# Copies of U and of first quarters ahead of seeds on ScalarE, p7's seed in two copies, p4's first quarter between p5's and p7's direct ones, and one check moved

## The chip, the cores and the metric

The kernel runs on one core of a Trainium2 chip. The engines in this text are TensorE (PE, with its weight loads listed as PEld), VectorE (DVE), ScalarE (ACT), GpSimd (POOL) and the queue of SyncE (SP), which issues transfers. Each engine takes its instructions strictly in the order in which they were written for it, and waits on semaphores for the work of the others. The metric is device microseconds of one execution; the kernel before took 794.69 us as the median of three runs (794.3 to 795.52).

## The reference

Two blocks follow each other. The first is attention with hashed buckets, for q, k and v of shape (4, 8, 768, 64): six sign bits of a projection give each query and key a bucket, and a score counts only where the buckets agree.

```python
scores = scale * np.matmul(q, k.transpose(0, 1, 3, 2))
scores = np.where(mask, scores, -1000000000.0)
attn = softmax(scores)            # with 1e-9 added to the sum
x = (attn @ v), heads side by side        # (4, 768, 512)
```

The second block is an MLP mixer over x. Every array is float32.

```python
h = np.maximum(xt @ w_tok1, 0.0) @ w_tok2         # xt: x with tokens last; 256 wide
u = x + h.transpose(0, 2, 1)
h2 = np.maximum(u @ w_ch1, 0.0) @ w_ch2           # 512 -> 1536 -> 512
return u + h2
```

The change lies in `np.maximum(u @ w_ch1, 0.0)`, for the last two of three parts of the tokens.

## The kernel before

The kernel has three stages: attention, the mixing of tokens, and the channels (function `channels`). In `channels` the 3072 tokens are taken in three parts `s` = 0, 1, 2 of 1024 tokens. Each part has a hidden stage (times w_ch1, then relu, into R0 to R3) and an output stage (`outputs`, times w_ch2).

Both products are formed by Winograd's variant of Strassen's scheme: seven block products p1 to p7 in the place of eight. For `s` = 1 and 2 the hidden stage applies the scheme twice. There one call of `hidden_first` (for t = 0) and two calls of `hidden_pair` (t = 1 and 2) make a part, so that `hidden_pair` runs four times in all. In a pair, p1 is computed whole and p2 to p7 are each an object of class `Smaller` with seven inner products of 128 x 256, in three methods:

- `one` forms the first inner product in PSUM and copies it to `e[:, 0]` with ScalarE (L925): the "first quarter".
- `rest` adds three more inner products in the same pair of PSUM banks. `finish` then copies the running sum U out of PSUM on ScalarE (L956), and VectorE adds it to the second and third quarters (L957) and forms the fourth (L961). The result is `e`, four quarters of 128 x 256.
- `three` forms the last three inner products, the "direct ones", and adds them to whatever stands in a given pair of PSUM banks.

So a quantity is complete when `e` and the direct ones have been added. In `hidden_pair` this is done for p6, p5 and p7 by putting a start value into the banks before `three` runs on them, the "seed". For p6 (bank pair Z) and p7 (bank pair V) the seed is `e` itself: `finish(to)` lets VectorE write the fourth quarter straight into the banks and then has ScalarE copy the first three quarters there in one copy of 128 x 768 (L963). For p5 (bank pair Y) VectorE adds `e5` and `u` into the banks (L981, function `plus`, line 1111).

Each matrix product of the program stands in the trace as two matmul instructions and two weight loads. In this text "p4's first quarter" on TensorE is thus a pair of instructions, and "p7's direct ones" are six. In the rows of the trace they can be told by what they read: p7's direct ones read `TA,WC` four times and `SW,WC` twice, p4's first quarter reads `TB,SW` twice, p5's direct ones read `TA,WC`, `TA,SW` and `second,WC` twice each.

There are eight PSUM banks, taken as four pairs. In `hidden_pair` they are named one to four: X and p3 use one, p5 and then Y use two, p2, p7 and p4 use three, Z and V use four.

The order of the work is written by hand: `tc.manual_schedule()` keeps, on each engine, the order of the program's statements, so that a statement that is moved in the text is moved on its engine's queue. Waits are put in by the framework from the tiles that are read and written. Weights for the inner products come by transfers on the SP queue; `used` issues the next one when `rest` and `three` of a quantity have both run.

One more thing is done on the side. A check (`look`: `begin_look` at L1444, `end_look` at L1452) loads one half of q or k with a transfer that POOL issues (L1462), squares it on ScalarE and adds up what lies over a bound, to decide at the end whether a careful path must run. There are 32 such loads with three under way at a time, so 35 calls drain them. The calls are spread over the hidden and output stages from the end of part 0 on; before the change there are 36, of which the last one has nothing to do.

Of the kernel before, what the change touches and what calls it, by code (L numbers as in the profile page):

```python
# [41 lines left out]
ALU = mybir.AluOpType  # L42
# [6 lines left out]
def kernel(  # L49
# [13 lines left out]
    nc = tc.nc  # L63
    P = 128
    B, NP, _, _, S = qk.shape
# [11 lines left out]
    TT = 512  # L77
# [674 lines left out]
    def channels(pool, psum, SW1, second, TA, judge):  # L752
# [7 lines left out]
        last = B * S // (2 * TT) - 1  # L760

        def copies():
            return pool.tile([P, 2 * TT], F32, name="c", tag="c", bufs=3)
# [4 lines left out]
        def bank_pair(i):  # L768
            return psum.tile([P, 2, TT], F32, name=f"b{i}", tag=f"b{i}", bufs=1)
# [91 lines left out]
        def split4(a):  # L861
            return a.rearrange("p (n t) -> p n t", n=4)
# [10 lines left out]
        def fetch_fifth(s, t):  # L873

            if t < GP:
                nc.sync.dma_start(
                    out=fifth_left().rearrange("p (i c) -> p i c", i=4),
                    in_=hidden_passed["p5"][:, :, P * t : P * t + P],
                )
# [26 lines left out]
        class Smaller:  # L906
# [11 lines left out]
                    w = hidden_left_at(h).rearrange("p (i c) -> p i c", i=7)  # L918
                    self.left = [w[:, i] for i in range(7)]

            def one(self, pair, e):

                self.ps, self.e = split4(pair.rearrange("p i n -> p (i n)")), split4(e)
                self.mm(self.ps[:, 0], 4, 0)
                nc.scalar.copy(self.e[:, 0], self.ps[:, 0])  # L925

            def three(self, pair, start=False):
# [21 lines left out]
            def mm(self, ps, left, right, start=True):  # L949
                accumulate(ps, lambda k: self.left[left], lambda k: self.b[right], [0], start)  # L950

            def finish(self, to=None):

                u = extra_flat()[:, TT // 2 * finished[0] : TT // 2 * (finished[0] + 1)]
                finished[0] = (finished[0] + 1) % 3
                nc.scalar.copy(u, self.ps[:, 0])  # L956
                nc.vector.tensor_tensor(  # L957
                    self.e[:, 1:3], self.ps[:, 1:3], u[:, None, :].to_broadcast([P, 2, TT // 2]), op=ALU.add,
                )
                last = self.e if to is None else split4(flat(to))  # L960
                nc.vector.tensor_tensor(last[:, 3], self.ps[:, 1], self.e[:, 2], op=ALU.add)  # L961
                if to is not None:
                    nc.scalar.copy(last[:, :3], self.e[:, :3])  # L963

        def parts_of(s, t):

            r = [a[:, :, t::GP].rearrange("p n i c -> p i n c") for a in R]
            h = 5 * GP * (s - 1) + 5 * t
            return r, [Smaller(h + i, name, s, t) for i, name in enumerate(SMALLER)]

        def rows(a):
            return a.rearrange("p (i n c) -> p i n c", i=2, n=2)
# [4 lines left out]
        def flat(a):  # L977
            return a.rearrange("p i n -> p (i n)")

        def plus(to, a, b):  # L980
            nc.vector.tensor_tensor(to, a, b, op=ALU.add)  # L981

        def copy_pair(to, pair):
            nc.scalar.copy(to.rearrange("p (i n) -> p i n", i=2), pair)
# [4 lines left out]
        def whole(pair, left, right, which, t):  # L989
            for i in which:  # L990
                at = P * (t + GP * i)
                accumulate(pair[:, i], lambda k: left(k)[:, at : at + P], right, range(KC))

        def opened(pair, which, s, t):
            start = TT * 2 * s
            whole(pair, lambda k: WC1[:, k], lambda k: XT[:, k, start : start + TT], which, t)
# [15 lines left out]
        def hidden_first(s, t, between):  # L1012


            r, (p2, p6, p7, p3, p4) = parts_of(s, t)
            x, z, e, y = ring
            ring[:] = [y, e, z, x]
            p1, e4, e2, e3 = [flat(output_at(i)) for i in range(4)]
            e7 = flat(q1)
            p5, e6, u = copies(), copies(), copies()  # L1020
            n = TT * 3 // 2

            X = bank_pair(x)
            opened(X, [0, 1], s, t)
            fetch_fifth(s, t + 1)
            Z, E = bank_pair(z), bank_pair(e)
            p2.one(E, e2)
            copy_pair(p1, X)
            p2.three(Z, True)
            Y = bank_pair(y)  # L1030
            whole(Y, lambda k: WC1[:, k, DCH // 2 :], lambda k: T[0][:, k], [0], t)
            plus(p1[:, :n], flat(Z)[:, :n], p1[:, :n])
            for job in between[:2]:
                job()
            p2.rest()
            whole(Y, lambda k: WC1[:, k, DCH // 2 :], lambda k: T[0][:, k], [1], t)
            p2.finish()
            copy_pair(p5, Y)
            plus(r[0], rows(p1), rows(e2))
            p6.three(X)  # L1040
            p6.one(bank_pair(z), e6)
            copy_pair(u, X)
            look()
            V = bank_pair(e)
            between[2]()
            p7.three(V, True)
            p6.rest()
            plus(p5[:, :n], flat(V)[:, :n], p5[:, :n])
            between[3]()
            p6.finish()  # L1050
            plus(u, u, e6)
            p7.one(bank_pair(x), e7)
            look()
            p3.three(Y)
            p7.rest()
            p7.finish()
            p3.one(bank_pair(z), e3)
            relu(r[0])
            p4.three(V)
            p3.rest()  # L1060
            plus(r[1], banks(Y), rows(u))
            plus(u, u, e7)
            plus(r[2][:, 0], banks(V)[:, 0], rows(u)[:, 0])
            plus(r[2][:, 1, 0], banks(V)[:, 1, 0], rows(u)[:, 1, 0])
            p3.finish()
            p4.one(bank_pair(x), e4)
            look()
            nc.scalar.copy(r[2][:, 1, 1], rows(u)[:, 1, 1])
            open_next(y, s, t)
            p4.rest()  # L1070
            plus(r[3], rows(p5), rows(u))
            p4.finish()
            plus(r[1], r[1], rows(e3))
            plus(r[2], r[2], rows(e4))
            look()
            later(r, (3, 2))

        def hidden_pair(s, t):


            r, (p2, p6, p7, p3, p4) = parts_of(s, t)
            p5 = Smaller(None, "p5", s, t)
            one, two, three, four = ring
            e2, e4, e5, e3 = [flat(output_at(i)) for i in range(4)]
            e6 = e7 = flat(q1)
            p1, u, v = copies(), copies(), copies()

            X = ahead.pop()
            p6.one(bank_pair(two), e6)
            opened(X, [1], s, t)  # L1090
            p2.one(bank_pair(three), e2)
            copy_pair(p1, X)
            p6.rest()
            p2.rest()
            Z = bank_pair(four)
            p6.finish(Z)
            p2.three(X)
            p2.finish()
            begin_look()
            p5.one(bank_pair(two), e5)  # L1100
            end_look()
            plus(r[0], banks(X), rows(e2))
            p6.three(Z)
            p7.one(bank_pair(three), e7)
            plus(u, flat(Z), p1)
            p5.rest()
            p5.finish()
            p3.one(bank_pair(one), e3)
            Y = bank_pair(two)
            plus(flat(Y), e5, u)  # L1110
            p7.rest()
            V = bank_pair(four)
            p7.finish(V)
            p3.rest()
            p5.three(Y)
            p3.finish()
            copy_pair(v, Y)
            p7.three(V)
            relu(r[0])
            plus(r[3], banks(V), rows(v))  # L1120
            p4.one(bank_pair(three), e4)
            p3.three(Y)
            relu(r[3])
            plus(r[1], banks(Y), rows(e3))
            p4.rest()
            p4.finish()
            look()
            p4.three(V)
            plus(e4, e4, u)
            plus(r[2], banks(V), rows(e4))  # L1130
            end_rows()
            if t + 1 < GP:
                open_next(one, s, t)
            else:
                ring[:] = [one, two, three, four]
            later(r, (2,))
# [5 lines left out]
        ahead, finished = [], [0]  # L1142
# [91 lines left out]
        def output_at(i):  # L1234

            at = 7 * QC * P + KC * TT * (i % 3)
            return area(i // 3)[:, at : at + KC * TT].rearrange("p (i n) -> p i n", i=KC)

        def extra_flat():
            at = 7 * QC * P + KC * TT  # L1240
            return area(1)[:, at : at + QC * TT // 2]
# [113 lines left out]
        def outputs(s):  # L1355
            sl = [slice(TT * (2 * s + i), TT * (2 * s + i) + TT) for i in range(2)]

            def add(to, a, b):
                return lambda: nc.vector.tensor_tensor(to, a, b, op=ALU.add)
# [15 lines left out]
            begin("p5")  # L1375
            combine("x", "r3", ALU.subtract, "r1", [(0, 0), (1, 0), (1, 1)])
            nc.scalar.copy(q1, ps)
            if s < last:
                look()
            q7, q57, q6, q5 = [output_at(i) for i in range(4)]  # L1380
            product(s, 1, "p5", q5, [lambda: combine("r0", "x", ALU.subtract, "r0")])
# [53 lines left out]
        def look():  # L1435
            begin_look()
            end_look()
# [192 lines left out]
```

## Time and profile before

| what | value |
|---|---|
| median of three runs | 794.69 us (794.3 to 795.52) |
| profiled execution, its own time | 795.07 us |
| its span, from the first to the last instruction | 793.2 us |
| PE busy | 785.3 us, 99% of the span |
| DVE, ACT, POOL busy | 674.4, 445.3 and 53.6 us |
| granted PE clock | 0.999 |
| the four calls of `hidden_pair` | from about 547.9, 570.4, 679.5 and 702.1 us on |

The page of a profile gives busy times and the chain of work that ended last. A row of the timeline gives the start and length in us, the engine, the line, the operation, what it writes and reads with shapes, how many instructions are merged in the row, and in brackets the idle time of that engine just before it with what ended it. Matmuls are pipelined: a matmul's recorded length overlaps the next, so that lost time on PE is read from the distances between starts.

### The profile page before, as it was taken

What the parts mean: (1) busy time and instruction counts of PE and PEld (TensorE: products, weight loads), DVE (VectorE), ACT (ScalarE), POOL (GpSimd) and SP (SyncE); (2) the same over time, 40 slices, a digit from 0 to 9 for tenths busy, and PEclk for the clock granted to TensorE, in tenths of its full rate; (3) what the DMA queues carried; (4) which work ended last, traced back from release to release, by engine and by line L of the source; (5) the groups of instructions that cost most, each with busy time, mean ns of one, the idle gap of its engine ahead of it and who ended that gap; (6) DMA issues with size and microseconds to landing.
All of it is one profiled execution on the core that took longest, in us unless ns stands there. A gap on an engine that the chain in (4) does not pass through costs nothing.

```text
span 793.2 us, 12404 instructions
## 1 busy us (share of the span) xinstructions
PE 785.3 (99%) x4721; PEld 475.2 (60%) x4721; DVE 674.4 (85%) x925; ACT 445.3 (56%) x726; POOL 53.6 (7%) x77
## 2 busy tenths in 40 slices
PE   9999999999999999999999999999999999999997
PEld 4444444444444444455544458877777887776886
DVE  5989898988987677999697789898779899878986
ACT  6688888888888886333323221327664555673111
POOL 1000000000000000011121010111000122000001
PEclk9999999999999999999999999999999999999999
DMA  4435353537452425795686995798745689720565
GB/s 164 163 123 163 123 163 123 163 125 240 148 181 88 150 47 167 216 263 111 119 279 234 347 371 164 225 302 240 250 141 197 236 236 245 232 84 0 190 172 123
DMA packets 102160, 144.85 MB, mean 183 GB/s; under 512 B 30216, under 2 KB 71888, under 8 KB 102096
## 3 DMA queue, kind: packets, MB, share of 16 engines
q1 hardware_dynamic: 93936, 119.02, 46.1%
q0 software_dynamic: 7728, 24.64, 13.6%
q8 instruction: 38, 0.62, 0.3%
q10 hardware_dynamic: 432, 0.34, 0.2%
q14 instruction: 26, 0.21, 0.1%
HBM read 101.01 MB, written 35.52 MB: 172 GB/s over the span
## 4 chain that ended last, share of the span: by engine, by line
PE 97%; DVE 2%; ACT 1%; issue 0%; ACTq 0%; DVEq 0%
PE b L780 48%; PE sc L353 20%; PE acc L407 16%; PE t L653 5%; PE t L693 5%; PE sums L431 2%; PE hp L301 1%; DVE b L981 1%; ACT b L963 0%; PE idle L470 0%; DVE second L957 0%; PE hw L325 0%; DVE q L957 0%; DVE b L961 0%; DVE second L961 0%; ACT second L956 0%
## 5 line engine op out<-in xcount | busy, mean ns | idle before, releaser
L360 ACT ACTIVATE e<-sc 128x768 f32<-128x768 f32 x192 | 154.2, 812 | 11.2 <-PE sc L353 10.8
L353 PE MATMUL sc<-qk 64*128 64x384 f32 x768 | 153.0, 484 | 0.0
L780 PE MATMUL b<-R,second 128*128 128x256 f32 (+1 forms) x612 | 150.9, 404 | 0.0
L780 PEld LDWEIGHTS b<-R,second 128*128 128x128 f32 x612 | 116.3, 190 | 31.6 <-issue 17.5
L407 PE MATMUL acc<-e,vn 128*32 128x384 f32 x1536 | 127.0, 486 | 0.0
L786 ACT COPY c<-b 128x512 f32<-128x512 f32 (+1 forms) x78 | 37.4, 488 | 156.6 <-PE b L780 142.7
L392 DVE TENSOR_TENSOR esd<-esd,e 128x768 f32<-128x768 f32 x96 | 92.0, 958 | 10.4 <-ACT e L360 0.5
L407 PEld LDWEIGHTS acc<-e,vn 128*32 128x32 f32 x1536 | 49.9, 110 | 73.9 <-issue 73.3
L353 PEld LDWEIGHTS sc<-qk 64*128 64x128 f32 x768 | 68.4, 188 | 41.8 <-issue 36.7
L780 PE MATMUL b<-XT,WC 128*128 128x256 f32 (+1 forms) x228 | 74.3, 470 | 0.0
L353 PE MATMUL sc<-bits 64*128 64x384 bf16 x384 | 62.5, 323 | 0.0
L780 PEld LDWEIGHTS b<-XT,WC 128*128 128x128 f32 x228 | 43.2, 190 | 25.9 <-issue 20.8
L388 DVE SCALAR_TENSOR_TENSOR esd<-e 128x768 f32<-128x768 f32 x32 | 30.6, 955 | 23.4 <-ACT e L360 23.4
L780 PE MATMUL b<-XT,SW 128*128 128x256 f32 (+1 forms) x156 | 43.7, 412 | 0.0
L653 PE MATMUL t<-x,W 128*128 128x512 f32 x96 | 41.8, 593 | 0.0
L353 PEld LDWEIGHTS <-bits 64*128 64x128 bf16 x384 | 18.5, 94 | 33.2 <-issue 9.4
L713 POOL DMA_DIRECT2D XT<-second x8 | 9.8, 1229 | 383.5 <-DVE second L712 361.2
L780 PEld LDWEIGHTS b<-XT,SW 128*128 128x128 f32 x156 | 29.6, 190 | 10.0 <-issue 5.1
L452 ACT COPY rec<-rec 32x384 f32<-32x384 f32 x64 | 32.6, 510 | 5.0 <-DVE rec L446 4.2
L413 ACT ACTIVATE num<-acc,vsum 128x384 f32<-128x384 f32 x32 | 18.6, 582 | 29.7 <-PE acc L407 29.3
L780 PE MATMUL b<-TA,WC 128*128 128x256 f32 (+1 forms) x92 | 34.0, 479 | 1.3 <-ACT b L963 1.3
L395 DVE TENSOR_TENSOR esd<-esd,e 128x768 f32<-128x768 f32 x32 | 30.5, 954 | 1.9
(243 smaller groups left out, 1172.5 us busy)
## 6 DMA issues: line engine op xcount, KB each, us to landing
second<-left SPq DMA_DIRECT2D x20, 768.0 KB
raw<-in_moe_w_ch SPq DMA_DIRECT2D x16, 768.0 KB
qk<-in_qk SPq DMA_DIRECT2D x15, 768.0 KB
second<-left SPq DMA_DIRECT2D x18, 576.0 KB
seen<-in_qk POOLq DMA_DIRECT2D x21, 384.0 KB, 4.8
WC<-hidden_left SPq DMA_DIRECT2D x18, 448.0 KB
vn<-in_v SPq DMA_DIRECT2D x16, 384.0 KB
vt<-in_vT SPq DMA_DIRECT2D x16, 384.0 KB
```

The source lines that it names most:

```text
L353: nc.tensor.matmul(sc[:, i, :HALF], t[rows, 1, P * c : P * c + P], t[rows, 0, qs], start=start, stop=not start,)
L360: nc.scalar.activation(e, sc[:, :, :HALF], ACT.Exp, scale=SCALE)
L388: nc.vector.scalar_tensor_tensor(self.d, es[0], NR * EPS, es[1], op0=ALU.add, op1=ALU.add,)
L392: nc.vector.tensor_tensor(self.d, self.d, e, op=ALU.add)
L395: nc.vector.tensor_tensor(self.d, self.d, self.es[-1], op=ALU.add)
L407: nc.tensor.matmul(acc[D * i + d : D * i + d + 32], vn[:, i, c, d : d + 32], e[:, i], start=(c == 0), stop=(c == NR - 1),)
L413: nc.scalar.activation(nums[self.n][:, self.half], acc, ACT.Identity, scale=-1.0, bias=vsum,)
L452: nc.scalar.copy(rec[other : other + 32, h], rec[at : at + 32, h])
L653: nc.tensor.matmul(ps, W1[:, r, P * j : P * j + P], x[:, r], start=(r == 0), stop=(r == NR - 1),)
L693: nc.tensor.matmul(ps[at], left, right, start=start, stop=True, skip_group_check=True,)
L780: nc.tensor.matmul(ps, left(k), right(k), start=start and k == ks[0], stop=stop and k == ks[-1], skip_group_check=True,)
L786: nc.scalar.copy(c, ps)
```

## The change

`finish` is split into `unite`, which copies U on ScalarE, and `add`, which holds the work of VectorE, with the fourth quarter written to a seed where one is given. The copy of the first three quarters into the seed is no longer part of it and stands in `hidden_pair`. `one` can leave its copy out, and `keep` does it later. In `hidden_pair`:

- p2's U is copied before the seed of p6 is.
- p7's seed is copied in two: the first quarter (128 x 256) right after p3's first quarter was copied, the other two (128 x 512) where the single copy stood. p3's U is copied before this second one.
- On TensorE, p4's first quarter stands between p5's direct ones and p7's direct ones. Before, it stood after p7's direct ones. Its copy to `e4` comes after that of Y to `v` on ScalarE.

The check at the end of `hidden_first` is taken out (for `s` = 1 and 2). The output stage of `s` = 1 begins with two checks in the place of one; that of `s` = 0 with one, as before. There are now 35 calls.

```diff
-            def one(self, pair, e):
+            def one(self, pair, e, now=True):
                 self.ps, self.e = split4(pair.rearrange("p i n -> p (i n)")), split4(e)
                 self.mm(self.ps[:, 0], 4, 0)
+                if now:
+                    self.keep()
+
+            def keep(self):
                 nc.scalar.copy(self.e[:, 0], self.ps[:, 0])
...
-            def finish(self, to=None):
-
-                u = extra_flat()[:, TT // 2 * finished[0] : TT // 2 * (finished[0] + 1)]
+            def unite(self):
+
+                self.u = extra_flat()[:, TT // 2 * finished[0] : TT // 2 * (finished[0] + 1)]
                 finished[0] = (finished[0] + 1) % 3
-                nc.scalar.copy(u, self.ps[:, 0])
+                nc.scalar.copy(self.u, self.ps[:, 0])
+
+            def add(self, last=None):
+
+                last = self.e if last is None else last
                 nc.vector.tensor_tensor(
-                    self.e[:, 1:3], self.ps[:, 1:3], u[:, None, :].to_broadcast([P, 2, TT // 2]), op=ALU.add,
+                    self.e[:, 1:3], self.ps[:, 1:3], self.u[:, None, :].to_broadcast([P, 2, TT // 2]), op=ALU.add,
                 )
-                last = self.e if to is None else split4(flat(to))
                 nc.vector.tensor_tensor(last[:, 3], self.ps[:, 1], self.e[:, 2], op=ALU.add)
-                if to is not None:
-                    nc.scalar.copy(last[:, :3], self.e[:, :3])
+
+            def finish(self):
+                self.unite()
+                self.add()
... in hidden_first
             plus(r[2], r[2], rows(e4))
-            look()
             later(r, (3, 2))
... in hidden_pair
             Z = bank_pair(four)
-            p6.finish(Z)
+            seed = split4(flat(Z))
+            p6.unite()
+            p6.add(seed)
+            p2.unite()
+            nc.scalar.copy(seed[:, :3], p6.e[:, :3])
             p2.three(X)
-            p2.finish()
+            p2.add()
...
             plus(u, flat(Z), p1)
+            V = bank_pair(four)
+            seed = split4(flat(V))
             p5.rest()
             p5.finish()
             p3.one(bank_pair(one), e3)
+            nc.scalar.copy(seed[:, 0], p7.e[:, 0])
             Y = bank_pair(two)
             plus(flat(Y), e5, u)
             p7.rest()
-            V = bank_pair(four)
-            p7.finish(V)
+            p7.unite()
+            p7.add(seed)
             p3.rest()
+            p3.unite()
+            nc.scalar.copy(seed[:, 1:3], p7.e[:, 1:3])
             p5.three(Y)
-            p3.finish()
+            p4.one(bank_pair(three), e4, False)
+            p3.add()
             copy_pair(v, Y)
+            p4.keep()
             p7.three(V)
             relu(r[0])
             plus(r[3], banks(V), rows(v))
-            p4.one(bank_pair(three), e4)
             p3.three(Y)
... in outputs
             nc.scalar.copy(q1, ps)
-            if s < last:
+            for _ in range(s + 1 if s < last else 0):
                 look()
```

## The prediction

> **What bounds the kernel now.** I read the page first. PE is busy 99% of the span and the chain that ended last is 97% PE, so only a stretch in which PE does not start its next matmul on time can be won, and any new one is lost whole.
>
> ```profile
> PE 785.3 (99%) x4721; PEld 475.2 (60%) x4721; DVE 674.4 (85%) x925; ACT 445.3 (56%) x726; POOL 53.6 (7%) x77
> PE 97%; DVE 2%; ACT 1%; issue 0%; ACTq 0%; DVEq 0%
> ```
>
> Next the waits of PE. In the channel stages one line ends PE's recorded idle time: the copy of a seed, four times, once in each `hidden_pair`.
>
> ```profile
> PE b L780 <- ACT b L963: 1.3, 4, 0.3
> ```
>
> 1.3 us is not the loss, since a matmul's length overlaps the next. I take the loss from the starts in the timeline of all engines, first pair of part 1:
>
> ```profile
> 558.18 0.37 ACT L956 COPY second<-b 128x256 f32<-128x256 f32 x1 [0.92 <-PE b L780]
> 558.59 0.69 DVE L957 TENSOR_TENSOR second<-b,second 128x512 f32<-128x512 f32 x1
> 559.31 0.42 DVE L961 TENSOR_TENSOR second<-b,second 128x256 f32<-128x256 f32 x1
> 559.71 1.46 PE L780 MATMUL b<-XT,SW 128*128 128x256 f32 x6
> 559.77 1.23 DVE L981 TENSOR_TENSOR b<-second,c 128x1024 f32<-128x1024 f32 x1
> 559.91 0.37 ACT L956 COPY second<-b 128x256 f32<-128x256 f32 x1 [0.92 <-PE b L780]
> 560.91 0.68 DVE L957 TENSOR_TENSOR q<-b,second 128x512 f32<-128x512 f32 x1
> 561.15 0.67 PE L780 MATMUL b<-TA,WC 128*128 128x256 f32 x2
> 561.63 0.43 DVE L961 TENSOR_TENSOR b<-b,q 128x256 f32<-128x256 f32 x1
> 562.09 0.59 PE L780 MATMUL b<-second,WC 128*128 128x256 f32 x2
> 562.15 0.80 ACT L963 COPY b<-q 128x768 f32<-128x768 f32 x1 [1.87 <-DVE b L961]
> 562.89 0.37 ACT L956 COPY second<-b 128x256 f32<-128x256 f32 x1
> 563.01 0.73 PEld L780 LDWEIGHTS b<-TA,WC 128*128 128x128 f32 x4 [0.73 <-ACT b L963]
> 563.01 1.13 PE L780 MATMUL b<-TA,WC 128*128 128x256 f32 x4 [0.33 <-ACT b L963]
> 563.98 0.59 PE L780 MATMUL b<-SW,WC 128*128 128x256 f32 x2
> ```
>
> Undisturbed, such matmuls start every 0.216 us (narrow ones; two make 0.43). From 562.09 p7's direct ones are due at 562.09 + 0.43 = 562.52, and their fifth instruction at 563.39; it starts at 563.98. So 0.59 us is lost, with the same spacing in the other three pairs. The weight load, which normally starts 0.216 ahead of its matmul, was due at 562.30 and came at 563.01, 0.71 late: 0.59 lost. At p5's direct ones (561.15) it is 0.33 late and 0.22 lost. Both say that the first 0.11 us of a late load costs nothing.
>
> The rows above it are the chain: p5's U (558.18), p5's sums, the seed Y (559.77), p7's sums, and the copy L963 for 0.80.
>
> The second loss is in the first pair after each `hidden_first`, from the timelines of ACT and PEld:
>
> ```profile
> 548.32 0.85 ACT L1444 ACTIVATE seen<-seen 128x768 f32<-128x768 f32 x1
> 550.13 0.35 ACT L925 COPY q<-b 128x256 f32<-128x256 f32 x1
> 550.54 3.75 PEld L780 LDWEIGHTS b<-XT,WC 128*128 128x128 f32 x18 [0.34 <-ACT q L925]
> ```
>
> A check holds the copy of p6's first quarter to 550.13, and p6's `rest` waits for that. PE's group of 24 instructions there takes 554.53 - 548.28 = 6.25 us to the next start; the same group of the second pair takes 576.91 - 570.87 = 6.04. Lost: 0.21, and 0.21 again in part 2 (6.24 against 6.03).
>
> **The change part by part.**
>
> *The check out of `hidden_first`.* p6's copy then starts when its matmul is done, about 548.48, and ends at 548.85; its `rest` is due at 550.43. Both losses go: -0.42 us. The next ACT work, p2's copy (550.63) and X's after it, waits for PE as before.
>
> *p2's U ahead of p6's seed.* In the second pair p2's `rest` ends near 575.78, so U runs from 575.81 to 576.18. The seed's copy could start at 576.17 before (VectorE's fourth quarter ended at 576.08), so it starts 0.01 later and ends near 576.98. With the 0.06 that L963 shows from its end (562.95) to PE's load, that load can start at 577.04; it is due at 577.12. Cost 0. If U pushed the seed by its whole 0.37, the load would be 0.29 late and 0.18 lost in each pair: +0.72 is the upper bound. p2's sums come 1.1 us earlier on VectorE; that wins nothing, since p5's sums wait for p5's own U (580.56), which waits for PE.
>
> *First quarter of p7's seed.* One more ACT instruction per pair. ACT reaches it after p3's first copy, at 558.98, and is idle for 0.92 before p7's U at 559.91. Its price lies between 0.37 (128x256, L956) and 0.80 (128x768, L963); either fits. It also waits until `plus(u, ...)` has read the banks, which ends at 558.55. Cost 0; if that cover went, p7's U still has 0.6 us, from 560.28 to VectorE's use of it at 560.91.
>
> *p3's U ahead of the rest of the seed.* p3's `rest` ends at 561.17, so U runs from 561.2 to 561.57, while ACT waited (1.87) before. Cost 0.
>
> *Rest of the seed.* The built order shows that it still waits for VectorE's fourth quarter, so it starts at 562.15. No row copies 128x512 from SBUF to PSUM; the bounds are 0.37 and 0.80 as above, and 0.59 (128x512 from PSUM, L786) is the nearest and lies on the line between them. It ends at 562.74 and lets the load go at 562.80.
>
> *p4's first quarter ahead of p7's direct ones.* It is 0.43 us of PE that was needed anyhow. It waits for p7's sums, which free its banks (VectorE, to 562.06), and for p4's weights, issued at 548.04; its load is due at 562.30. It moves p7's direct ones to 562.95 and their load to 562.74. The load goes at 562.80, 0.06 late, inside the free 0.11: nothing lost. So the whole 0.59 goes, in four pairs: -2.37. With 0.37 it is the same; with 0.80 the load is 0.27 late, 0.16 is lost and 1.72 is won. The split alone would leave 0.39 of the 0.59; the move alone 0.16. The two together are what clears it.
>
> A rule of the Trainium skill speaks against the split. "ScalarE: Activation LUTs", section "What ACT_TABLE_LOAD costs", gives an instruction without pointer operands 186 ns plus 0.833 ns per element: 826 ns for 768 elements (the row has 800), 399 and 613 for the two copies, so 0.19 us more ScalarE work. By the page the second copy would end at 562.76 and the load would start 0.08 late, still free, and the sum would be the same.
>
> *What stands behind.* p3's direct ones, now due at 564.25 (load 564.03), need Y copied to `v`: that copy (1.02, 563.16 before) starts when p5's direct ones are done, near 562.75, and ends at 563.77. `keep` follows to 564.1; p4's `rest` needs it at 565.55. p4's direct ones need `plus(r3)`, which waits for p7's and ends near 565.65; they are due at 566.85. The 0.22 at p5's direct ones stays: its chain is untouched. SP and POOL issue in the same order.
>
> *Two checks at the output stage of part 1.* From the timelines of ACT and PE:
>
> ```profile
> 602.51 0.85 ACT L1444 ACTIVATE looked<-looked 128x768 f32<-128x768 f32 x1
> 604.33 0.35 ACT L786 COPY c<-b 128x256 f32<-128x256 f32 x1
> 606.58 7.93 PE L780 MATMUL b<-R,second 128*128 128x256 f32 x36
> ```
>
> A check takes 1.82 from 602.51 to the next instruction. A second one moves the copy to 606.14 and its end to 606.49. PE adds to that bank at 606.58; its load is due at 606.37 and would go at 606.55, 0.18 late: +0.07. Bounds 0 and 0.3 (were the check to take 2.0). Later checks find loads issued one check later, POOL's median landing is 4.8 us (page), and the nearest, issued at 604.8, is read at 610.2. In part 2 the last check becomes real, behind the second pair; part 1 has the same check there (590.33) and PE's next start, 605.29, is on time.
>
> Sum: -0.42 - 2.37 + 0.07 = -2.72 us. The profiled execution (795.07, of which 793.2 span) would take 792.35. It stands 0.38 above the median of the runs, 794.69, from which I get 792.0.
>
> **The rivals.** *Part of the gain only* (0.11). The second copy takes 0.80: -0.42 - 1.72 + 0.07 = -2.07, 792.6; with p2's U in the way as well, 793.3. For it: the margin is 0.05. Against: ACT's lengths follow the width everywhere (0.37, 0.59, 0.80).
>
> *The stall moves on* (0.07). The wait reappears at p3's direct ones, behind Y's copy, at the old price of 0.59: only the checks' part remains, -0.35, 794.3. Against: that copy has 0.26 to the load and 0.11 free.
>
> *Slower* (0.06): the first quarter's copy blocks ACT. It is the one new wait on VectorE in that queue, and p7's U, p3's U, the second copy and Y's copy stand behind it. It costs nothing until it ends after 560.1, and makes the kernel 1.6 us slower, 796.3, when each pair loses 0.59 + 0.49 = 1.08, thus from an end near 561.7. For that `plus(u)` would have to end more than 2 us later than 558.55, and its inputs come earlier now.
>
> *As forecast* (0.76).
>
> **How the numbers follow.** 0.2% (1.6 us) is about what a measurement of this kernel can tell from no change. Faster are the forecast and the partial gain: 0.87. The moved stall lies within 0.2%: 0.07. Slower: 0.06. The low end takes 0.6 off the forecast for the spread of a median of such runs (794.3 to 795.5); the high end is the partial gain with p2's U in the way, 793.3, and 0.2 for the two checks. The range is 791.4 to 793.5.
>
> **What would show it.** In the profile after: no PE wait on a seed's copy; p7's direct ones 0.43 after p4's first quarter with no gap; the first pair's group of 24 at 6.04; a second copy of 0.59; 0.22 still lost at p5's direct ones; up to 0.1 lost at p5's product in the output stage of part 1. I am wrong if PE waits for the second copy, for Y's copy or for p4's first quarter.

## The result, and the profile after

The changed kernel takes 792.09 us (median of six runs, 791.4 to 792.45) against 794.82 for the kernel before in the same comparison: a ratio of 0.9964, with a 95% interval of 0.9951 to 0.9977. The forecast was 792.0. The profiled execution took 792.34 us with a span of 790.5.

The page, first the busy times and then the chain that ended last:

```profile
PE 782.9 (99%) x4721; PEld 475.6 (60%) x4721; DVE 674.3 (85%) x925; ACT 446.5 (56%) x730; POOL 53.5 (7%) x77
PE 98%; DMA 1%; SPq 0%; DVE 0%; issue 0%
```

PE's recorded busy time fell by 2.4 us with the same number of instructions. Of this, 1.45 us lies in the channel stages, where lost time is in part recorded as busy (before, the four matmuls at 563.01 have 1.13 us, and after, the same four have 1.03). The rest lies ahead of those stages, where nothing was changed and PE's busy time goes from 385.3 to 386.3 us among the profiles of this text. ACT is no longer named in the chain, and DVE's share of it fell from 2% to 0%. ACT has four instructions more, one in each `hidden_pair`. In the list of who waited for whom, PE now waits for nothing in the channel stages, though the sums below still find 0.93 us lost there.

The first pair of part 1 in the timelines of PE, PEld, ACT and DVE (start, length, line, operation; line numbers are those of the changed kernel, where L1123 is the first quarter of p7's seed, L1131 the rest of it, L960 a copy of U and L993 the copy of Y):

```profile
561.88 0.59 PE L780 MATMUL b<-second,WC 128*128 128x256 f32 x2
562.31 0.59 PE L780 MATMUL b<-TB,SW 128*128 128x256 f32 x2
562.74 1.03 PE L780 MATMUL b<-TA,WC 128*128 128x256 f32 x4
563.61 0.59 PE L780 MATMUL b<-SW,WC 128*128 128x256 f32 x2
562.59 0.78 PEld L780 LDWEIGHTS b<-TA,WC 128*128 128x128 f32 x4
558.68 0.38 ACT L1123 COPY b<-q 128x256 f32<-128x256 f32 x1
561.00 0.37 ACT L960 COPY second<-b 128x256 f32<-128x256 f32 x1 [0.92 <-PE b L780]
561.95 0.59 ACT L1131 COPY b<-q 128x512 f32<-128x512 f32 x1 [0.57 <-DVE b L968]
562.51 1.01 ACT L993 COPY c<-b 128x1024 f32<-128x1024 f32 x1
561.42 0.43 DVE L968 TENSOR_TENSOR b<-b,q 128x256 f32<-128x256 f32 x1
```

The four PE rows follow each other at 0.43, 0.43 and 0.87: there is no gap where 0.59 was lost. p4's first quarter (562.31) stands in front of p7's direct products (562.74). Their weight load was due at 562.53 and went at 562.59, 0.06 late, and nothing was lost.

The first pair's group of 24 instructions behind `hidden_first`, with the next row, from the timeline of PE:

```profile
548.29 6.20 PE L780 MATMUL b<-XT,WC 128*128 128x512 f32 x24
554.32 0.59 PE L780 MATMUL b<-TA,WC 128*128 128x256 f32 x2
```

It takes 6.03 us to the next start, 6.25 before. The output stage of part 1, with two checks, from the timeline of all engines:

```profile
601.12 0.85 ACT L1462 ACTIVATE seen<-seen 128x768 f32<-128x768 f32 x1
602.93 0.83 ACT L1462 ACTIVATE looked<-looked 128x768 f32<-128x768 f32 x1
604.72 0.35 ACT L786 COPY c<-b 128x256 f32<-128x256 f32 x1
605.12 7.64 PEld L780 LDWEIGHTS b<-R,second 128*128 128x128 f32 x36 [0.18 <-ACT c L786]
605.19 7.98 PE L780 MATMUL b<-R,second 128*128 128x256 f32 x36
```

The copy behind the checks ends at 605.07 and the load goes at 605.12, late by 0.15. It costs 0.04, read from the starts (the row is 7.98 long, against 7.93 before).

For all kernels below I add up the time that PE loses from 440 us on: the distance from each matmul's start to the next, less 0.216 for a narrow and 0.432 for a wide one. Only distances of more than 0.025 over it count.

| kernel | p6 behind `hidden_first`, 2 places | p5's direct products, 4 places | p7's direct products, 4 places | p5's product in the output stage of part 1 | sum, us |
|---|---|---|---|---|---|
| before | 0.21 each | 0.22 each | 0.59 each | 0 | 3.68 |
| after | 0 | 0.22 | 0 | 0.04 | 0.93 |

The difference is 2.75 us. That no loss lies elsewhere can be seen from the whole stretch, from the start of the first matmul of the channel stages to the end of the last: 400.33 us before, 397.58 after, again 2.75 less. For each of the eight kernels below, too, this stretch differs from that of the kernel before by the difference of the sums, within 0.01 us.

The medians differ by 2.73, but the interval of the ratio stands for anything from 1.8 to 3.9 us. That the medians come so close to the forecast is in part luck; the sums are the evidence.

### The profile page after: what moved, and what is told of

It reads as the page before. It is cut to its first block, busy times and chain, and to the rows that moved or that the text cites. A ratio compares the mean times of both kernels' runs of the same rounds, so it can differ in the third digit from the quotient of the medians.

```text
span 790.5 us, 12412 instructions
## 1 busy us (share of the span) xinstructions
PE 782.9 (99%) x4721; PEld 475.6 (60%) x4721; DVE 674.3 (85%) x925; ACT 446.5 (56%) x730; POOL 53.5 (7%) x77
## 4 chain that ended last, share of the span: by engine, by line
PE 98%; DMA 1%; SPq 0%; DVE 0%; issue 0%
PE b L780 50%; PE sc L353 20%; PE acc L407 16%; PE t L653 5%; PE t L693 5%; PE sums L431 2%; PE hp L301 1%; DMA qk<-in_qk 1%; PE hw L325 0%; SPq L271 0%; DVE second L1365 0%; PE b L1492 0%; SPq L1643 0%
```

## The experiments

Spans are a poor judge of tenths here. The first matmul of the channel stages starts anywhere from 386.5 to 387.9 us in these profiles, which no edit touches. So the sums of lost time decide, and the timed ratios stand beside them.

**The check alone.** The kernel before, with nothing but the check moved.

```diff
             plus(r[2], r[2], rows(e4))
-            look()
             later(r, (3, 2))
...
-            if s < last:
+            for _ in range(s + 1 if s < last else 0):
                 look()
```

> The kernel before with only the check moved. My theory (each late weight load costs its lateness less 0.11 us, place by place): the two losses of 0.21 us behind hidden_first go, 0.04 comes at p5's product in the output stage of part 1, and the four losses of 0.59 us in front of p7's direct products stay as they are. Span 793.2 - 0.38 = 792.8 us. Rival (the check is what held ScalarE, and so the seeds too): the four losses go as well, span near 790.5.

Ratio to the kernel before 0.9998 (0.9989 to 1.0008). The times alone could not tell this kernel from the one before. In the trace the two losses of 0.21 are gone, 0.04 appears at p5's product, and the four of 0.59 stand unchanged: a sum of 3.29, 0.39 less than before. PE's list of waits still has the seed:

```profile
PE b L780 <- ACT b L963: 1.3, 4, 0.3
```

The rival falls. The seeds do not wait because the check holds ScalarE.

**The pair alone.** The changed kernel with the check back at the end of `hidden_first`.

```diff
             plus(r[2], r[2], rows(e4))
+            look()
             later(r, (3, 2))
...
-            for _ in range(s + 1 if s < last else 0):
+            if s < last:
                 look()
```

> The changed kernel with the check put back at the end of hidden_first. Theory: the four losses of 0.59 us go, the two of 0.21 stay: span 793.2 - 2.37 = 790.8 us. Rival (the pair's new order needs the free ScalarE): the first pair of each part still waits for its seed, span 791.4 or more.

Ratio 0.9969 (0.9958 to 0.9980). The four losses of 0.59 are gone, the two of 0.21 remain: a sum of 1.30, 2.38 less than before. The timeline of PEld has the late load behind the check:

```profile
549.81 2.24 PEld L780 LDWEIGHTS b<-XT,WC 128*128 128x128 f32 x11 [0.34 <-ACT q L929]
```

The rival falls: with the check in its old place, no pair waits for its seed. With the check alone that makes 0.39 + 2.38 = 2.77 against 2.75 for both together, so the two halves of the change are independent within 0.02 us.

**The split alone.** p4's first quarter back behind p7's direct products.

```diff
-            p4.one(bank_pair(three), e4, False)
             p3.add()
             copy_pair(v, Y)
-            p4.keep()
             p7.three(V)
             relu(r[0])
             plus(r[3], banks(V), rows(v))
+            p4.one(bank_pair(three), e4)
             p3.three(Y)
```

> The changed kernel with p4's first quarter back behind p7's direct products, its copy with it. Theory: the second copy of the seed still lets the load go 0.06 after its end, but the load is due 0.43 earlier, 0.49 late, 0.38 lost in each of four pairs: span 790.5 + 1.5 = 792.0 us. Rival A (the shorter copy does it all): 790.5. Rival B (the split does nothing): 0.59 lost each, 792.9.

Ratio 0.9983 (0.9973 to 0.9993). From the timeline of all engines:

```profile
561.64 0.59 PE L780 MATMUL b<-second,WC 128*128 128x256 f32 x2
561.70 0.59 ACT L1131 COPY b<-q 128x512 f32<-128x512 f32 x1 [0.58 <-DVE b L968]
562.34 0.73 PEld L780 LDWEIGHTS b<-TA,WC 128*128 128x128 f32 x4 [0.51 <-ACT b L1131]
562.34 1.13 PE L780 MATMUL b<-TA,WC 128*128 128x256 f32 x4
563.31 0.59 PE L780 MATMUL b<-SW,WC 128*128 128x256 f32 x2
```

The load was due at 561.64 + 0.43 - 0.216 = 561.85 and went at 562.34, 0.49 late; 0.38 is lost in each pair, the sum is 2.44. Both rivals fall. Note that the PE row has no bracket: the loss does not show as idle time.

**The move alone.** p7's seed in one copy again.

```diff
-            nc.scalar.copy(seed[:, 0], p7.e[:, 0])
...
-            nc.scalar.copy(seed[:, 1:3], p7.e[:, 1:3])
+            nc.scalar.copy(seed[:, :3], p7.e[:, :3])
```

> The changed kernel with p7's seed in one copy of 128x768, where the second copy stood. Theory: the copy ends 0.21 later, the load is 0.28 late, 0.17 lost in each of four pairs: span 790.5 + 0.7 = 791.2 us. Rival A (the move does it all): 790.5. Rival B (a late load costs its whole lateness): 0.28 each, 791.6.

Ratio 0.9971 (0.9959 to 0.9982). From the timeline of all engines:

```profile
561.36 0.80 ACT L1130 COPY b<-q 128x768 f32<-128x768 f32 x1 [0.57 <-DVE b L968]
561.73 0.59 PE L780 MATMUL b<-TB,SW 128*128 128x256 f32 x2
562.21 0.73 PEld L780 LDWEIGHTS b<-TA,WC 128*128 128x128 f32 x4 [0.29 <-ACT b L1130]
562.21 1.13 PE L780 MATMUL b<-TA,WC 128*128 128x256 f32 x4
563.18 0.59 PE L780 MATMUL b<-SW,WC 128*128 128x256 f32 x2
```

The load was due at 561.73 + 0.43 - 0.216 = 561.94 and went 0.27 late; 0.16 is lost in each pair (563.18 - 562.21 is 0.97 in the place of 0.86, and 0.05 stands before it). The sum is 1.56. A load that is 0.27 late costs 0.16: rival A (nothing lost) and rival B (0.27 lost) both fall.

**U behind the seeds.** p2's and p3's U after the seeds' copies, as before the change.

```diff
-            p2.unite()
             nc.scalar.copy(seed[:, :3], p6.e[:, :3])
+            p2.unite()
...
-            p3.unite()
             nc.scalar.copy(seed[:, 1:3], p7.e[:, 1:3])
+            p3.unite()
```

> The changed kernel with p2's U and p3's U again behind the seeds' copies. Theory: both were free where they stood; Y's copy ends 0.2 later and its load is still on time: no loss, span 790.5 us. Rival (the order of the U copies is part of what clears the wait): some of the 0.59 comes back in each pair, span 791 to 792.9.

Ratio 0.9963 (0.9950 to 0.9975). The sum is 0.92, that of the changed kernel. Copying U ahead of the seeds wins nothing in this kernel: ScalarE had the time either way. The rival falls.

**The second copy twice.**

```diff
-            nc.scalar.copy(seed[:, 1:3], p7.e[:, 1:3])
+            for _ in range(2):
+                nc.scalar.copy(seed[:, 1:3], p7.e[:, 1:3])
```

> The changed kernel with the second copy of p7's seed done twice. Theory: the margin is used up, so the repeat (about 0.52 us on ScalarE) shows nearly whole: load 0.58 late, 0.47 lost in each of four pairs, span 790.5 + 1.9 = 792.4 us. Rival (there is more room than the margin of 0.05 us): less than 0.3 lost each, span under 791.7.

Ratio 0.9995 (0.9985 to 1.0004). From the timeline of all engines:

```profile
562.15 1.21 ACT L1132 COPY b<-q 128x512 f32<-128x512 f32 x2 [0.58 <-DVE b L968]
562.52 0.59 PE L780 MATMUL b<-TB,SW 128*128 128x256 f32 x2
563.41 0.73 PEld L780 LDWEIGHTS b<-TA,WC 128*128 128x128 f32 x4 [0.70 <-ACT b L1132]
564.38 0.59 PE L780 MATMUL b<-SW,WC 128*128 128x256 f32 x2
```

The repeat cost 0.62, not the 0.52 that I expected: the two copies, which write the same place, take 1.21 together, without the overlap that I had assumed. The load was due at 562.73 by the unrounded starts and went at 563.41, 0.68 late; 0.57 is lost in each pair, and the sum is 3.21. The loss is again the lateness less 0.11, the rival falls, and one more copy of this size takes back 2.28 of the 2.75 us.

**The first copy three times as wide.** Its last two quarters are written again by the second copy.

```diff
-            nc.scalar.copy(seed[:, 0], p7.e[:, 0])
+            nc.scalar.copy(seed[:, :3], p7.e[:, :3])
```

> The changed kernel with the early copy of p7's seed at 128x768 in place of 128x256 (its last two quarters are written again by the second copy). Theory: it takes 0.80 in place of 0.38 in a stretch in which ScalarE waits 0.64 for PE: no loss, span 790.5 us. Rival (the early copy blocks the queue before p7's U): up to 0.43 lost in each pair, span up to 792.2.

Ratio 0.9963 (0.9951 to 0.9976). From the timeline of all engines, the early copy and p7's U behind it:

```profile
559.23 0.81 ACT L1123 COPY b<-q 128x768 f32<-128x768 f32 x1
560.26 0.37 ACT L960 COPY second<-b 128x256 f32<-128x256 f32 x1 [0.22 <-PE b L780]
```

0.81 in place of 0.38, and ScalarE still waits 0.22 for PE. The sum is 0.93: nothing lost. The rival that the early copy blocks the queue falls.

**Three checks.** One more at the start of the output stage of part 1.

```diff
-            for _ in range(s + 1 if s < last else 0):
+            for _ in range(2 * s + 1 if s < last else 0):
                 look()
```

> The changed kernel with three checks in place of two at the start of the output stage of part 1 (the last call of all then has nothing to do). Theory: two checks just fit (0.04 lost), the third shows whole at p5's product: 1.8 us more, span 792.3. Rival (ScalarE has room there, the 0.04 is something else): no more than 0.1, span 790.6.

Ratio 0.9986 (0.9976 to 0.9995). From the timeline of all engines, the third check, the copy behind it and the load:

```profile
604.64 0.83 ACT L1462 ACTIVATE seen<-seen 128x768 f32<-128x768 f32 x1
606.43 0.84 ACT L786 COPY c<-b 128x256 f32<-128x256 f32 x2
606.83 3.32 PEld L780 LDWEIGHTS b<-R,second 128*128 128x128 f32 x16 [1.97 <-ACT c L786]
```

1.84 us is lost at this one place, for a sum of 2.72. Two checks fit there but for 0.04 us; the third costs 1.80 more, its whole length. The rival falls.

| kernel | at p7's direct products, each of 4 | sum lost, us | against before | forecast for the run |
|---|---|---|---|---|
| check alone | 0.59 | 3.29 | -0.39 | -0.38 |
| pair alone | 0 | 1.30 | -2.38 | -2.37 |
| split alone | 0.38 | 2.44 | -1.24 | -1.2 |
| move alone | 0.16 | 1.56 | -2.12 | -2.0 |
| U behind | 0 | 0.92 | -2.75 | -2.7 |
| second copy twice | 0.57 | 3.21 | -0.47 | -0.8 |
| first copy wide | 0 | 0.93 | -2.74 | -2.7 |
| three checks | 0 | 2.72 | -0.96 | -0.9 |

(The last column is the span that was expected for each, less 793.2; for the first two, the difference as it was written.)

## Why the prediction was right, point by point

- *The check out of `hidden_first`*, forecast -0.42: the loss of 0.21 is gone in both parts. Shown by the check alone.
- *p2's U ahead of p6's seed*, forecast 0: right, shown by the kernel with both U's back in their old places. In the trace after, U runs 553.23 to 553.60 and the seed's copy starts at 553.58, as the working had it for the second pair.
- *First quarter of the seed*, forecast 0 between 0.37 and 0.80: 0.38 measured, and no loss even at 0.81.
- *p3's U*, forecast 0: right, by the same run as p2's.
- *Rest of the seed*, forecast 0.59 by the nearest row and 0.06 from there to the load: 0.59 and 0.05 measured. "ScalarE: Activation LUTs" of the Trainium skill, section "What ACT_TABLE_LOAD costs", would give 0.40 and 0.61 for the two copies; the trace has 0.38 and 0.59. What follows from its figures, that a split costs more ScalarE work, holds: the two copies take 0.97 us together, where the single one took 0.80. It cost nothing, since ScalarE was waiting in those places.
- *p4's first quarter ahead*, forecast -2.37 in four pairs: 4 x 0.59 = 2.37 gone. That neither half does it alone was forecast as 0.39 left by the split alone and 0.16 by the move alone; 0.38 and 0.16 were measured.
- *What stands behind*: p3's direct products were on time, and the 0.22 at p5's direct products stayed in all four pairs.
- *Two checks*, forecast +0.07: 0.04. The two checks took 3.60 from 601.12 to the copy at 604.72, where the working had 3.63.

What carried the forecast is the lateness of one weight load: 0.71 before, less 0.43 by the move and 0.21 by the split, which leaves 0.07; 0.06 was measured. Neither alone is enough, as the runs show. The rule read from two places of the trace, that the first 0.11 us of a late load is free, decides the rest: without it the 0.06 would cost 0.24 us in the four pairs, and the move alone and the split alone would lose 0.27 and 0.49 in each pair instead of 0.16 and 0.38. The working had 0.05 us of room before the gain would begin to shrink, and I gave the partial gain 0.11 for that reason. The runs put the rule to the test at loads 0.06, 0.15, 0.27, 0.49 and 0.68 late: 0, 0.04, 0.16, 0.38 and 0.57 were lost. A load of the kernel before that was 0.11 late (it went at 556.15, for the matmul at 556.25) lost nothing. Why the first 0.11 is free, no run here tells.

One bound in the working of the rival "slower" is off: an early copy costs nothing until it ends near 560.5, not 560.1, by the 0.6 us of room for p7's U that the same working gives (559.91 + 0.6). The sum does not use it, and no run came near it: with the copy of 768 elements ScalarE still had 0.22 to spare.

What is left: 0.88 us at p5's direct products. Their chain (U, two sums, the seed Y) was not shortened by any run.

## What to carry to other kernels

Where PE is the bound, take what a wait costs from the distances between starts, and compare the weight load's start with the time at which it was due. Two small edits that each leave part of a wait can clear it together, when one brings the awaited work earlier and the other puts needed work of the bound engine in front; cost each against the same due time before adding. Work put on an engine that is idle in that place is free until it meets the next due time, and then it shows whole, as the third check did.

## What the runs showed that was not expected

PE's list of waits is blind to small losses. With the split alone PE loses 1.5 us in four places (0.38 each), and with the move alone 0.6 us, and the list names no wait for ScalarE in either; the smallest loss at a seed that it names is 0.57, as 0.30 us idle. PEld's rows show these waits as idle time, but do not always name the cause. At p5's direct products, where 0.22 is lost in every kernel, the timeline of PEld after the change has

```profile
560.91 0.30 PEld L780 LDWEIGHTS b<-TA,WC 128*128 128x128 f32 x2 [0.35 <-issue]
```

and only the due time shows the loss. Two copies by ScalarE to the same place took 1.21 us, twice the 0.59 of one and a little more; no run shows why. By contrast, neighbours with different targets overlap somewhat (558.41 to 558.68 in the trace after, for a copy of 0.37).
